# Transposes by the upper and lower half of the TensorE array, in a linear-attention and expert network

## The chip, the cores and the metric

The kernel runs on one core of one Trainium2 chip. The metric is the device time of one execution in microseconds (us). TensorE's matmuls are called PE here and its weight loads PEld; VectorE is DVE, ScalarE is ACT, GpSimd is POOL, and SP is the queue that issues the DMAs.

## The reference

Two kinds of layer alternate, A B A B, on x of 2048 tokens by 576 features, each with a layer norm ahead and a residual behind:

```python
x = x + A(layernorm(x), wqkv, wo)      # 32 heads of 18, linear attention
x = x + B(layernorm(x), w_q, k1, k2, u, v)
x = x + A(layernorm(x), wqkv, wo)
x = x + B(layernorm(x), w_q, k1, k2, u, v)

# A: q, k, v = x @ wqkv;  pq, pk = phi(q), phi(k)
#    kv = sum_s pk v^T;  z = sum_s pk;  o = (pq kv) / (pq z);  return o @ wo
# B: scores of 32 heads against 8 + 8 keys, best of each: one of 64 experts per head
#    return sum over heads of gelu(x . u[e]) * v[e]        (the softmax over one is 1)
```

Everything is fp32.

## The kernel before, in words

Tokens are worked on in 16 tiles of 128 (`NT`), so that a tile has its tokens on the 128 partitions and its features along the free axis. A matmul wants the features on the partitions, so each tile is transposed three times in each pair of layers: the layer-norm output before q, k and v (`front_T`, called `fT` in the written order, PSUM tile `ptf`), the scaled q features before the output product (`back_oT`, `oT`, `pto`), and the layer-norm output before the expert scores (`exp_T`, `bc`, `ptb`). `exp_T` also transposes the 128 x 128 tile of expert weights `cg` of an earlier token tile, mostly in the same call. All go through `transposed` (line 190): five blocks of 128 columns (`NB`), six with `cg`, each one `nc.tensor.transpose` (line 197) that loads the block of y, o or cg as the weights and streams the identity through, into columns of a PSUM tile of 1024 columns (two banks of 512). A second step, after a `yield`, splits the PSUM tile into `hi` and `lo` (`split`, lines 102 and 103): ACT writes the rounded fp32r copy, DVE the rest that it leaves. The products (`product` at line 212, `back_out` at 402, `exp_scores` at 433, `exp_out` at 517) then use `hi` and `lo` as weights in fp32r, so that three passes together give nearly fp32.

The other matmuls are `front_state` (lines 283 and 285, fp32, `kva`), which sums pk v^T over the tiles, and, in the first pass over the tiles, `fold_mm` (line 550), which multiplies the queries' weights by the keys. `fold_mm` is the one place where the array is used in parts: each of its weights has 32 columns, and four of them stand side by side in column groups of 32. In each tile of that stage, eight `fold_mm` come in one bunch.

The order of the work is written out by hand: `play` and `step2` list the pieces, `run` resumes a piece up to its next `yield`, and `in_order` ties every engine's instructions to that order. In the middle (`step2`, token tiles 5 to 12, one step for each) the first layer B of tile s, its output `po`, the second layer A's k and v of tile s - 3 and the transposes of tile s - 2 run in one step. There, `bc`, `fT` and `oT` stand near each other: `bc` and `fT` back to back on PE (eleven transposes), then `front_state`, then `oT` (five).

Of the kernel before, what the change touches and what calls it, by code (L numbers as in the profile page):

```python
# [22 lines left out]
P = 128  # L23
# [34 lines left out]
def network(ctx, tc, x_in, wqkv, wo, wq_t, k_t, u_t, v2, c_mask, c_mask4, c_ident, c_code, c_code1, c_scale, c_shift, out):  # L58
    nc = tc.nc
# [6 lines left out]
    def psum(name):  # L66
        return ps.tile([P, 1024], F32, tag="ps", name=name)
# [5 lines left out]
    ident = cp.tile([P, P], F32, name="ident")  # L73
# [26 lines left out]
    def split(src, hi, lo, eng=nc.vector):  # L100

        nc.scalar.activation(hi, src, AF.Copy)  # L102
        eng.tensor_tensor(lo, src, hi.bitcast(F32), op=ALU.subtract)  # L103
# [86 lines left out]
    def transposed(y, n, more=None, tag="t", step=P):  # L190

        todo = [y[:, b * step:b * step + P] for b in range(NB)] if y is not None else []
        todo += [] if more is None else [more]
        w = len(todo) * P
        pt = psum(f"pt{n}")
        for b, x in enumerate(todo):
            nc.tensor.transpose(pt[:, b * P:(b + 1) * P], x, ident)  # L197
        nb = NB if tag == "t" else NB + 1
        hi = wk.tile([P, nb, P], F32R, tag=tag + "hi", name=f"thi{n}", bufs=4 if tag == "t" else 1)
        lo = wk.tile([P, nb, P], F32R, tag=tag + "lo", name=f"tlo{n}", bufs=4 if tag == "t" else 1)  # L200
        yield
        split(pt[:, :w], hi.rearrange("p a b -> p (a b)")[:, :w], lo.rearrange("p a b -> p (a b)")[:, :w])
        return hi, lo

    def product(tt, hi, lo, cols, n, cut=HALF, rem=REM, by_block=False):
# [25 lines left out]
    def front_T(l, t):  # L231
        tt["f", l, t] = yield from transposed(ys.pop(("f", l, t)), f"f{l}_{t}")
# [151 lines left out]
    def back_oT(l, t):  # L384
        hi, lo = tt["oT", l, t] = yield from transposed(tt.pop(("o", l, t)), f"o{l}_{t}", step=HC)
        nc.gpsimd.tensor_copy(lo[96:112, 4], hi[:16, 4].bitcast(F32))
# [26 lines left out]
    def exp_T(l, t, c):  # L413

        y = ys.pop(("b", l, t)) if ok(t) else None
        cg = tt.pop(("cg", l, c)).rearrange("p a b -> p (a b)") if ok(c) else None
        if y is None and cg is None:
            return
        hi, lo = yield from transposed(y, f"b{l}_{t % 99}", cg, tag="t" if cg is None else "u")
        if y is not None:  # L420
            tt["b", l, t] = hi, lo
        if cg is not None:
            b = 0 if y is None else NB
            tt["c", l, c] = hi[:, b], lo[:, b]
# [426 lines left out]
```

## Time and profile before

| | |
|---|---|
| median of 3 runs | 755.47 us (755.28 to 756.19) |
| the profiled execution | 754.99 us, of which its span is 753.2 us |
| granted TensorE clock, mean | 0.999 |
| PE busy, PEld busy | 98%, 92% of the span |
| DVE, ACT, POOL busy | 61%, 38%, 26% |
| mean busy share of DMA queue 1 | 32% |

The span is the time from the first instruction to the last. PE is busy nearly throughout. Matmuls overlap in the profile: each lasts some 0.27 to 0.50 us from its start to its end, while the next starts 0.06 to 0.24 us after it. So what PE spends on one is read from the distance of the starts (called the pitch below), not from the duration. A weight load is shown with its own start; it runs beside the matmul before it. In a row of the timeline, the second number is the time from the start of the first instruction of a merged group to the end of its last.

### The profile page before, as it was taken

How to read it: one execution, taken by the hardware profiler on the slowest of the kernel's cores; microseconds unless marked ns; L12 is line 12 of the kernel's file. 1: busy time of each engine (PE TensorE's matmuls, PEld its weight loads, DVE VectorE, ACT ScalarE, POOL GpSimd, SP SyncE). 2: the span in 40 equal slices, each digit the busy share in tenths (PEclk: the TensorE clock that was granted, in tenths of full speed). 3: DMA queues.
4: the chain of work that ended last, by engine and by line, in shares of the span. 5: the costliest groups of instructions: out<-in, count | busy, mean ns of one | idle time of the engine just before them, and what ended most of it. 6: DMA issues, size and time to landing. Idle time of an engine off the chain costs nothing. (4 is left out here: it accounts for less than half of the span.)

```text
span 753.2 us, 13998 instructions
## 1 busy us (share of the span) xinstructions
PE 735.4 (98%) x5356; PEld 692.9 (92%) x5356; DVE 459.0 (61%) x1008; ACT 289.0 (38%) x586; POOL 197.1 (26%) x540
## 2 busy tenths in 40 slices
PE   7999999999999999999999999999999999999995
PEld 5999989999998989999999999999999999999984
DVE  5532342324246887666666666464366899899986
ACT  5422232232333544444444444353233333444343
POOL 2110001000002543333333333130033334533431
PEclk9999999999999999999999999999999999999999
DMA  9737446641111322322232212221734323121101
GB/s 272 248 100 243 162 169 220 220 119 49 48 63 32 111 84 82 98 84 83 87 103 105 88 67 76 90 72 51 187 86 118 103 83 114 32 84 44 48 33 63
DMA packets 52267, 79.48 MB, mean 106 GB/s; under 512 B 5480, under 2 KB 22376, under 8 KB 52200
## 3 DMA queue, kind: packets, MB, share of 16 engines
q1 hardware_dynamic: 52200, 78.59, 32.0%
q8 instruction: 42, 0.69, 0.4%
q14 instruction: 25, 0.20, 0.1%
HBM read 55.01 MB, written 23.56 MB: 104 GB/s over the span
## 5 line engine op out<-in xcount | busy, mean ns | idle before, releaser
L219 DVE TENSOR_SCALAR ek<-ek 128x576 f32<-128x576 f32 x32 | 14.7, 459 | 83.6 <-ACT ek L218 83.6
L212 PE MATMUL ppk<-whi,thif 128*128 128x288 f32 x320 | 50.2, 301 | 1.9 <-ACT thif L102 1.9
L402 PE MATMUL ppo<-ohi,thio 126*128 126x288 f32 (+1 forms) x320 | 50.7, 300 | 0.1
L212 PEld LDWEIGHTS ppk<-whi,thif 128*128 128x128 f32 x320 | 44.2, 188 | 5.9 <-issue 3.3
L163 POOL TENSOR_SCALAR rsf<-mvf 128x1 f32<-128x1 f32 x16 | 3.1, 192 | 175.7 <-DVE mvf L161 175.6
L212 PE MATMUL ppk<-whi,tlof 128*128 128x288 f32 x320 | 48.7, 296 | 0.2 <-DVE tlof L103 0.2
L219 DVE TENSOR_SCALAR eq<-eq 128x576 f32<-128x576 f32 x32 | 15.6, 488 | 54.2 <-ACT eq L218 54.2
L212 PE MATMUL ppv<-whi,thif 128*128 128x252 f32 x320 | 48.1, 296 | 0.1
L212 PE MATMUL ppv<-whi,tlof 128*128 128x252 f32 x320 | 47.6, 295 | 0.0
L187 ACT ACTIVATE yb<-x,rsb 128x640 f32<-128x640 f32 x32 | 29.5, 923 | 43.4 <-POOL rsb L180 43.3
L433 PE MATMUL pps<-shi,thib 128*128 128x512 f32 x160 | 44.0, 405 | 1.9 <-ACT thib L102 1.9
L402 PEld LDWEIGHTS ppo<-ohi,thio 126*128 126x128 f32 (+1 forms) x320 | 44.8, 189 | 0.9 <-DVE eq L221 0.3
L212 PEld LDWEIGHTS ppk<-whi,tlof 128*128 128x128 f32 x320 | 44.6, 188 | 0.5 <-DVE tlof L103 0.5
L212 PEld LDWEIGHTS ppv<-whi,tlof 128*128 128x128 f32 x320 | 44.7, 188 | 0.0
L212 PEld LDWEIGHTS ppv<-whi,thif 128*128 128x128 f32 x320 | 44.3, 188 | 0.4 <-ACT thif L102 0.3
L173 ACT ACTIVATE junk<-x,mb 128x576 bf16<-128x576 f32 x32 | 24.7, 771 | 49.7 <-POOL mb L172 46.4
L433 PE MATMUL pps<-shi,tlob 128*128 128x512 f32 x160 | 42.4, 395 | 0.0
L245 ACT ACTIVATE v<-ppv 128x252 f32<-128x252 f32 x64 | 20.9, 380 | 55.0 <-PE ppv L212 55.0
L218 ACT ACTIVATE eq<-ppq 128x576 f32<-128x576 f32 x32 | 20.7, 647 | 52.1 <-PE ppq L212 52.1
L212 PE MATMUL ppq<-whi 128*128 128x288 f32 x260 | 39.9, 300 | 0.6 <-DVE eq L221 0.6
L402 PE MATMUL ppo<-ohi,tloo 126*128 126x288 f32 x256 | 40.3, 295 | 0.0
L402 PE MATMUL ppo<-olo,thio 126*128 126x288 f32 x256 | 40.3, 296 | 0.0
(156 smaller groups left out, 1797.7 us busy)
## 6 DMA issues: line engine op xcount, KB each, us to landing
fold<-in_wq_t SPq DMA_DIRECT2D x64, 288.0 KB, 5.3
whi<-hl_d SPq DMA_DIRECT2D x26, 320.0 KB, 3.9
pq_d<-eq SPq DMA_DIRECT2D x19, 288.0 KB, 2.1
pq<-pq_d SPq DMA_DIRECT2D x19, 288.0 KB, 2.8
xf<-in_x SPq DMA_DIRECT2D x16, 288.0 KB, 5.6
x<-in_x SPq DMA_DIRECT2D x16, 288.0 KB, 2.8
x_d<-x SPq DMA_DIRECT2D x16, 288.0 KB, 3.0
x<-x_d SPq DMA_DIRECT2D x16, 288.0 KB, 2.8
```

The lines of the kernel that those rows point to most:

```text
L163: nc.gpsimd.tensor_scalar(rs[:, 0:1], mv[:, 1:2], EPS_LN, 1.0, op0=ALU.add, op1=ALU.mult)
L173: nc.scalar.activation(junk, xt, AF.Square, bias=m[:, 0:1], accum_out=m[:, 1:2])
L187: nc.scalar.activation(y, x2, AF.Identity, scale=rs[:, 0:1], bias=rs[:, 1:2])
L212: nc.tensor.matmul(o[:, at:at + c1 - c0], tt[a == "lo"][:, b, :], wb[:, cols + c0:cols + c1], start=(i == 0), stop=(i == len(todo) - 1))
L218: nc.scalar.activation(e.rearrange("p (b c) -> p b c", b=2), halves(p), AF.Exp)
L219: nc.vector.tensor_scalar(e, e, 1.0, EPS, op0=ALU.min, op1=ALU.add)
L245: nc.scalar.activation(vt[:, c * w:(c + 2) * w].rearrange("p (c e) -> p c e", c=2)[:, :, :HC], x.rearrange("p (c e) -> p c e", c=2), AF.Copy)
L402: nc.tensor.matmul(p[:, h * 512:h * 512 + HALF], hl[a][:r, b], w[:r, h * HALF:(h + 1) * HALF], start=(i == 0), stop=(i == len(todo) - 1))
L433: nc.tensor.matmul(p[:, :512], hl[a == "lo"][:, b, :], shi[:, b] if w == "hi" else slo[:, blocks(REM)[b][1]], start=(i == 0), stop=(i == l ...
```

## The change

The transposes of `transposed` are cut in two by token. Where one instruction transposed a block of 128 tokens by 128 features, there are now two, one for tokens 0 to 63 with the upper left 64 x 64 corner of the identity, one for tokens 64 to 127 with the lower right corner. Each loads 64 rows by 128 columns as weights, streams 64 columns, and gives 128 features by 64 tokens. Each stands in one half of the array's rows: in the built program these instructions have a tile of 64 rows by 128 columns at row 0 or 64, where all others but `fold_mm` have 128 by 128. The upper half writes into the first bank of the PSUM tile, the lower half into the second. The split reads the two banks as (half, block, 64) and writes `hi` and `lo` in their old layout, in runs of 64 elements. The transposes of `fold_T` (line 565) are left as they were, and the order of the pieces on every engine is the same.

```diff
         todo += [] if more is None else [more]
-        w = len(todo) * P
+        n_b = len(todo)
+
         pt = psum(f"pt{n}")
         for b, x in enumerate(todo):
-            nc.tensor.transpose(pt[:, b * P:(b + 1) * P], x, ident)
+            for h in range(2):
+                r = slice(64 * h, 64 * h + 64)
+                nc.tensor.transpose(pt[:, h * 512 + b * 64:h * 512 + b * 64 + 64], x[r], ident[r, r])
...
         yield
-        split(pt[:, :w], hi.rearrange("p a b -> p (a b)")[:, :w], lo.rearrange("p a b -> p (a b)")[:, :w])
+
+        def dst(x):
+            return x[:, :n_b].rearrange("p b (h t) -> p h b t", h=2)
+
+        split(pt.rearrange("p (h b t) -> p h b t", h=2, t=64)[:, :, :n_b], dst(hi), dst(lo))
         return hi, lo
```

## Rows read from the trace of the kernel before

**Rows 1.** The page, busy time of each engine, share of the span, instructions.
```profile
PE 735.4 (98%) x5356; PEld 692.9 (92%) x5356; DVE 459.0 (61%) x1008; ACT 289.0 (38%) x586; POOL 197.1 (26%) x540
```
**Rows 2.** Line 197: duration in ns, min/median/max, first and last start in us, shapes.
```profile
L197 PE MATMUL ptf<-ident,yf x160: 270/272/327, 7.2 to 524.4; 128*128 128x128 f32 x160
L197 PE MATMUL pto<-ident,o x160: 270/272/300, 237.0 to 722.5; 128*128 128x128 f32 x160
L197 PE MATMUL ptb<-ident,yb x160: 270/272/330, 249.0 to 736.8; 128*128 128x128 f32 x160
L197 PE MATMUL ptb<-ident,cg x32: 270/273/331, 265.7 to 747.7; 128*128 128x128 f32 x32
```
**Rows 3.** Timeline of PE in one middle step: start us, us, engine, line, operation, count.
```profile
337.88 0.71 PE L197 MATMUL ptb<-ident,yb 128*128 128x128 f32 x5
338.43 0.27 PE L197 MATMUL ptb<-ident,cg 128*128 128x128 f32 x1
338.54 0.71 PE L197 MATMUL ptf<-ident,yf 128*128 128x128 f32 x5
339.08 1.05 PE L283 MATMUL kva<-ek,v 128*127 128x126 f32 x8
...
340.10 0.71 PE L197 MATMUL pto<-ident,o 128*128 128x128 f32 x5
340.64 1.43 PE L433 MATMUL pps<-shi,thib 128*128 128x512 f32 x5
```
**Rows 4.** Timeline of PEld, loads of transposes after a wait.
```profile
300.40 0.14 PEld L197 LDWEIGHTS ptb<-ident,yb 128*128 128x128 f32 x1 [0.44 <-ACT yb L187]
300.46 0.25 PEld L197 LDWEIGHTS ptb<-ident,yb 128*128 128x128 f32 x2
```
**Rows 5.** Timeline of PE into and through a bunch of `fold_mm`, several narrow windows.
```profile
49.55 0.29 PE L285 MATMUL kva<-ek,v 128*73 128x72 f32 x2
49.62 0.23 PE L285 MATMUL kva<-ek,v 128*73 128x72 f32 x1
49.77 0.46 PE L550 MATMUL fold_ps<-fold,kpad 128*32 128x320 f32 x1
49.77 0.50 PE L550 MATMUL fold_ps<-fold,kpad 128*32 128x320 f32 x4
49.77 2.18 PE L550 MATMUL fold_ps<-fold,kpad 128*32 128x320 f32 x32
51.31 0.65 PE L550 MATMUL fold_ps<-fold,kpad 128*32 128x256 f32 x8
51.52 0.44 PE L550 MATMUL fold_ps<-fold,kpad 128*32 128x256 f32 x4
```
**Rows 6.** Timeline of PE and PEld out of that bunch, several narrow windows.
```profile
51.89 0.40 PE L212 MATMUL ppk<-whi,thif 128*128 128x288 f32 x1
51.89 0.19 PEld L212 LDWEIGHTS ppk<-whi,thif 128*128 128x128 f32 x1 [0.41 <-issue]
52.13 0.43 PE L212 MATMUL ppk<-whi,thif 128*128 128x288 f32 x2
52.13 0.56 PE L212 MATMUL ppk<-whi,thif 128*128 128x288 f32 x3
```
**Rows 7.** Waits of PEld: total us, times, longest us.
```profile
PEld ppk L212 <- issue: 3.3, 8, 0.4
```
**Rows 8.** Waits of PE: total us, times, longest us.
```profile
PE ptb L197 <- DVE cg L498: 2.5, 2, 1.7
PE pps L433 <- ACT thib L102: 1.9, 3, 1.0
```
**Rows 9.** ACT by line and shape: busy us, mean ns; idle before and its releaser.
```profile
L102 ACT ACTIVATE thif<-ptf 128x640 fp32r<-128x640 f32 x32 | 22.6, 706 | 10.0 <-PE ptf L197 10.0
L245 ACT ACTIVATE v<-ppv 128x252 f32<-128x252 f32 x64 | 20.9, 380 | 55.0 <-PE ppv L212 55.0
L572 ACT ACTIVATE shi<-fold_pt 128x112 fp32r<-128x112 f32 x20 | 4.8, 417 | 11.7 <-PE fold_pt L565 11.7
L102 ACT ACTIVATE thib<-ptb 128x128 fp32r<-128x128 f32 x5 | 1.4, 277 | 6.3 <-PE ptb L197 6.3
```

## The prediction

> **What bounds the kernel now.** I read the share of each engine first, then the transposes' own line, then the timeline of PE where transposes stand, and last the one place where the array already changes its partition. PE is busy 98% of the span with 5356 matmuls and no other engine is over 61% [rows 1], so what PE spends or saves is, to first order, time. PE's waits on other engines are few: the two largest sums are 2.5 and 1.9 us [rows 8].
>
> What a transpose costs is its pitch. In a middle step five transposes start at 337.88 and the next instruction at 338.43, five more at 338.54 and the next at 339.08 [rows 3]: 0.109 us each, and nothing ahead or behind, because PEld runs ahead of PE. There are 160 + 160 + 160 + 32 = 512 of them [rows 2], so 512 x 0.109 = 55.8 us, 7% of the span. In the written order of PE they stand in 81 unbroken runs: 45 of five, 15 of eleven, 13 of six, 4 of ten, 4 of one. The step of [rows 3] has an eleven and a five.
>
> The load of a transpose is quicker than its matmul: after a wait the first load starts at 300.40 and the second at 300.46 [rows 4], so one occupies PEld for about 0.059 us, and the matmul sets the pitch.
>
> **What the rows say of an array in parts.** `fold_mm` is the row nearest to what the change makes. Two things are seen. First, parts do work at the same time: four matmuls on four column groups start within 0.04 us (0.50 for four, 0.46 for one), and 32 matmuls of 320 and 256 columns are through in 2.18 us [rows 5]; the last four, of 256 columns, took 0.21 us each from 51.31 to 51.52, and 32 of those in a line would be 6.7 us. The loads of the four groups are hidden as well.
>
> Second, going into that partition and out of it costs PE time. In: the second L285 has 0.06 us of columns (0.29 for two, 0.23 for one), so PE is free at 49.68, but the first `fold_mm` starts at 49.77: 0.095 us lost [rows 5]. Out: the last `fold_mm` starts at 51.58 (0.44 for four, 0.38 for one), has 0.21 us of columns, and is done at 51.79. The next product's load starts only at 51.89, although its weights were ready, and the profile says "issue" for the 0.41 us in which PEld stood [rows 6]. The same stands 8 times, 3.3 us in all [rows 7], once per bunch. Since the load could not run ahead, it lies bare too: the second product matmul starts 0.24 us after the first, where the pitch is 0.13 (0.56 less 0.43) [rows 6]. So out costs 0.095 + 0.105 = 0.20 us.
>
> The Trainium skill, "TensorEngine Tiling (Array Packing)", section Key Properties, says that changing the tiling mode drains TensorE, and names no price; it speaks of every mode, a row mode too, and so against this change. By it the two losses above come at each run of transposes; without it they would not, which is the third rival below.
>
> **The change, part by part.** *Matmuls and loads:* 512 transposes become 1024, each half as many rows and half as many streamed columns, each with a load of 128 columns. If the halves work side by side as column groups do, a pair has the pitch of one half. No row shows a row group, so I bound the pair: from below by half of 0.109, 0.055 us, since 64 columns are streamed for 128; from above by two loads one after the other, 2 x 0.059 = 0.118. Between, the pair can't be quicker than a load, 0.059, if loads of a half set the pitch. I take 0.057, between 0.055 and 0.059, since in [rows 5] loads of different groups ran at once; the upper end is a rival. 512 x (0.057 - 0.109) = **-26.6 us**. The second half starts some 0.013 us after the first (0.04 for three more [rows 5]): 81 x 0.013 = **+1.1 us**.
>
> *Into the new partition,* 81 times: 0.095, and the first load bare, 0.059: 81 x 0.154 = **+12.5 us**. No row shows this for a half; the ends are nothing (0) and what `fold_mm` shows, and I take the latter, it being the only row.
>
> *Out of it,* 81 times: 0.095, and a bare load of the fp32 or fp32r operand behind, 0.105: 81 x 0.20 = **+16.2 us**, with the same ends.
>
> *Split:* ACT and DVE read two runs of PSUM and write ten or twelve runs of 64. Two runs cost ACT nothing: the v copy, 252 elements in two runs, is 380 ns, and the line through 277 ns for 128 elements and 706 for 640 gives 381 [rows 9]. Sixteen runs of seven scattered elements do cost: 417 ns for 112, where that line gives 264, so 0.0096 per run [rows 9]. For ten runs of 64 the ends are 0 and 0.1 us a split. I take 0, because 64 elements in one run are nearer to the v copy's 126 than to scattered ones. It would lie beside PE's other work except where PE waits for a split, as in [rows 8]; at worst I allow 3 us for it.
>
> *Order, queues, waits:* no piece moves on any engine, no DMA is added, and each run still waits for the same y, o or cg at its first load, and is released to ACT at its last matmul.
>
> *The sum:* -26.6 + 1.1 + 12.5 + 16.2 = +3.2 us. By the length of a run: a run of five saves 0.26 and pays 0.37, a run of eleven saves 0.57 and pays 0.37. Break-even is at seven, and 62 of 81 runs are shorter. Where PE stands anyway beside a run, a switch hides in the wait; I count some dozen such ends, 6 x 0.095 + 6 x 0.20 = 1.8 us. But time that a long run saves ahead of a wait is lost there too: in the middle step PE needs thib right behind the second run, and thib comes from ACT [rows 3, 8]. So I keep a third, -0.6. That makes **+2.6 us**: 757.6 against the profiled execution's 754.99, and 758.1 against the median, 755.47, which is 0.5 higher. I give 758.1.
>
> **Rivals.** *No pairing* (slower by much): the halves share one path for loads, so that the two loads of 0.059 come one after the other and the pair takes as long as the whole did, about 0.11. Then the body saves nothing and the switches are paid in full: 1.1 + 12.5 + 16.2 = 29.8, less about 4 that PE's waits swallow, so +26, about 781 us. It decides if the pair's pitch is over about 0.09. For it: only column groups are seen to load at once. Against it: nothing in the rows makes halves of the rows more alike than column groups. The Trainium skill, "TensorE: Matmul & The Clock Gate", section "LDWEIGHTS (loading the stationary operand)", says that a load's time goes by its columns and not by its rows, so that two loads of 64 rows are twice the work of one of 128; by it this rival is the outcome if loads do not pair, and the trace shows no load of fewer rows at the same columns to test it. Chance 0.20.
>
> *A pair in between,* 0.07 to 0.085, as the loads overlap in part: 512 x 0.02 = 10 more, about 766. Chance 0.09.
>
> *No drain, or a cheap one, for a row partition* (faster): the columns of a 64 x 128 tile leave the array as before, so that the switch costs little and loads run ahead. At 0 the body's -26.6 would be the whole change on PE, but the middle step can't use it, since there PE meets ACT's thib right behind the runs [rows 3, 8]; I keep 10 to 15 of it as an estimate: 740 to 746. Against: eight bunches, both ends, show the loss [rows 7]. The point from which it decides is a switch of in and out together below 0.31 us, where I count 0.354. At 0.07 instead of 0.095 for the drains the sum falls by 4.1 to -1.5, about 754. Chance 0.13.
>
> *The change does not do what it says* (a half is put through as a full tile, with neither pairing nor drain) would give the first rival's body without its switches, no change at all; the tile sizes in the built program speak against it, and I leave it inside the "same" chance.
>
> **How the numbers follow.** A measurement here tells 0.2%, 1.5 us, from no change. The forecast (pairs at 0.055 to 0.060, drains as in `fold_mm`) has 0.58; its own range is 753 to 763: the drains at 0.07 and the pair at 0.055 below, the split's 3 us and 0.060 above. In it lie 0.37 slower, 0.16 same, 0.05 faster. The no-pairing rival and the pair in between add 0.29 to slower. Cheap drains split 0.02 same and 0.11 faster. So slower 0.66, same 0.18, faster 0.16. The forecast's range alone holds under 0.6, so the range reaches up to the no-pairing rival: 752.8 to 782.
>
> **What would show it.** In the profile after: PE and PEld with 5868 instructions each; at a run of five pairs, about 0.29 us from the first of the ten to the last plus a tail; about 0.1 us between the end of the columns before and the first load of a run, and the same behind it, as "issue" waits at some 80 places; the second matmul behind a run 0.24 us after the first. L102 and L103 at their old 0.7 and 0.8 us. Wrong at once if ten halves take 0.5 us or more (no pairing), or if loads behind a run start before its last matmul (no drain).

## The result, and the profile after

The changed kernel takes 757.54 us (median of 16 runs), the kernel before 755.53 in the same measurement: a ratio of 1.0026, with a 95% interval of 1.0019 to 1.0032. It is 2.0 us slower, where 2.6 were forecast; the profiled execution has a span of 754.8 us.

The page, busy time of each engine, as in [rows 1]:

```profile
PE 736.3 (98%) x5868; PEld 677.9 (90%) x5868; DVE 459.0 (61%) x1008; ACT 288.0 (38%) x586; POOL 196.7 (26%) x540
```

PE and PEld have the 5868 instructions foreseen, and the other engines are where they were. The line of the transposes (now 200), against [rows 2]: 

```profile
L200 PEld LDWEIGHTS ptb<-ident,yb x320: 134/139/142, 250.3 to 738.4; 64*128 64x128 f32 x160
L200 PE MATMUL ptb<-ident,yb x320: 221/223/273, 250.3 to 738.5; 64*128 64x64 f32 x160
```

A load of 64 rows lasts as long as one of 128 did (median 139 ns; 0.14 us in [rows 4], and 140 ns as the median of line 197): the half has half the columns to stream, but a whole load.

The timeline of PE in the same middle step as [rows 3]:

```profile
339.51 0.53 PE L200 MATMUL ptb<-ident,yb 64*128 64x64 f32 x10
339.87 0.23 PE L200 MATMUL ptb<-ident,cg 64*128 64x64 f32 x2
339.93 0.47 PE L200 MATMUL ptf<-ident,yf 64*128 64x64 f32 x10
340.34 1.15 PE L290 MATMUL kva<-ek,v 128*127 128x126 f32 x8
341.32 0.29 PE L292 MATMUL kva<-ek,v 128*73 128x72 f32 x2
341.55 0.53 PE L200 MATMUL pto<-ident,o 64*128 64x64 f32 x10
342.17 0.51 PE L440 MATMUL pps<-shi,thib 128*128 128x512 f32 x1
```

From the first transpose to the state matmuls, the eleven now take 0.83 us, where they took 1.20. But the way in and the way out stand beside them. Narrow windows of the same stretch, PE and PEld:

```profile
339.26 0.31 PE L219 MATMUL ppv<-whi,tlof 128*128 128x324 f32 x1
339.50 0.13 PEld L200 LDWEIGHTS ptb<-ident,yb 64*128 64x128 f32 x1 [0.17 <-issue]
339.50 0.20 PEld L200 LDWEIGHTS ptb<-ident,yb 64*128 64x128 f32 x3 [0.17 <-issue]
339.51 0.27 PE L200 MATMUL ptb<-ident,yb 64*128 64x64 f32 x2
339.62 0.41 PE L200 MATMUL ptb<-ident,yb 64*128 64x64 f32 x7
...
340.12 0.29 PE L200 MATMUL ptf<-ident,yf 64*128 64x64 f32 x4
340.33 0.18 PEld L290 LDWEIGHTS kva<-ek,v 128*127 128x127 f32 x1
340.34 0.48 PE L290 MATMUL kva<-ek,v 128*127 128x126 f32 x2
```

**Pair.** The second pair starts at 339.62, the seventh (the first of ptf) at 339.93: 0.31 for five steps, 0.063 us a pair. The two matmuls of a pair start about 0.003 us apart: the first two take 0.27 us together, and one alone takes 0.27.

**In.** The last product matmul starts at 339.26; one of 324 columns takes 0.148 (the distance from such a start to the next among the product matmuls), so PE is free at 339.41. The first load starts at 339.50, 0.09 later, and it lies bare.

**Out.** The last half starts at 340.18 (0.29 for four, 0.22 for one) and has 0.053 of columns (a quarter of the 0.21 for 256 columns in [rows 5], an estimate), so it is through at 340.24. The next load starts at 340.33, again 0.097 later, and the second state matmul at 340.55 (0.48 for two, 0.27 for one), 0.21 behind the first, where it was 0.11 in the kernel before. This is the picture of `fold_mm` in [rows 5, 6], at a partition into row halves.

The waits of PEld show the way in at 57 of the 81 runs; the row of [rows 7] stands unchanged beside three others:

```profile
PEld ptb L200 <- issue: 6.3, 25, 1.9
PEld ppk L219 <- issue: 3.3, 8, 0.4
PEld pto L200 <- issue: 3.2, 13, 0.4
PEld ptf L200 <- issue: 3.2, 19, 0.2
```

They are 25 + 13 + 19 = 57 places with 12.7 us of "issue" ahead of the runs, some of it in waits that were there before. The prediction looked for some 80 places, and the same behind the runs; the pause behind a run is not in this list and is read from the starts alone.

The price of a run can be read without a model, from the start of the same matmul in the two profiles. For each of the 81 runs I took how much later the second matmul behind it starts, less how much later the last one ahead of it did:

| length of the run | runs | median change, us | sum, us |
|---|---|---|---|
| 1 | 4 | +0.19 (from -0.06 to +0.31) | +0.6 |
| 5 | 45 | +0.10 | +2.9 |
| 6 | 13 | +0.06 | +0.5 |
| 10 | 4 | -0.13 | -0.4 |
| 11 | 15 | -0.175 | -2.3 |

Together +1.3 us. Two of the fives stand in the first 15 us, at the warm-up matmuls and the first loads of weights, and make -1.1 of it, which I don't read as the price of a run: that stretch moves by as much without any change in it (the kernel with halves in the long runs, below, whose transposes are all whole up to 249 us, stands 1.2 us behind the kernel before at 30 us). From 30 us on, the runs add 2.3 us, the stretches between them take back 0.7, and the last matmul starts 1.6 us later.

All the lengths from five on agree on one price: with 0.046 saved per whole transpose, 0.10 + 5 x 0.046, 0.06 + 6 x 0.046 and 11 x 0.046 - 0.175 are each 0.33 to 0.34 us for a way in and out. Break-even is between seven and eight transposes.

### The profile page after: what moved, and what is told of

Read it like the earlier page. It is cut to its first block, busy times and chain, and to the rows that moved or that the text cites. A ratio compares the mean times of both kernels' runs of the same rounds, so it can differ in the third digit from the quotient of the medians.

```text
span 754.8 us, 15025 instructions
## 1 busy us (share of the span) xinstructions
PE 736.3 (98%) x5868; PEld 677.9 (90%) x5868; DVE 459.0 (61%) x1008; ACT 288.0 (38%) x586; POOL 196.7 (26%) x540
## 5 line engine op out<-in xcount | busy, mean ns | idle before, releaser
L398 DVE SCALAR_TENSOR_TENSOR x<-po,x 128x576 f32<-128x576 f32 x29 | 21.9, 754 | 30.8 <-PE po L524 29.7
L445 ACT ACTIVATE s<-pps 128x512 f32<-128x512 f32 x32 | 19.1, 596 | 56.2 <-PE pps L440 56.1
```

The costliest lines, as they stand in the source:

```text
L398: nc.vector.scalar_tensor_tensor(y.rearrange("p (b c) -> p b c", b=2), halves(p), 0.0, xt.rearrange("p (b c) -> p b c", b=2), op0=ALU.add, ...
L445: nc.scalar.activation(s[:, NE:], p[:, :512], AF.Copy)
```

## The experiments

The theory is that the change is the sum of a saving per transpose and a price per run of them. Its rivals are that the loss comes from the split's new order or from more instructions; that pairing is worth nothing; and that the way in and out costs nothing. Each kernel was timed beside the kernel before.

**The split alone.** Whole transposes, read in the new order:

```diff
-        split(pt[:, :w], hi.rearrange("p a b -> p (a b)")[:, :w], lo.rearrange("p a b -> p (a b)")[:, :w])
+        split(pt[:, :n_b * P].rearrange("p (b h t) -> p h b t", h=2, t=64), dst(hi), dst(lo))
```

> The kernel before with one edit: the split reads and writes in the order half, block, 64, from whole transposes. Theory (the change in time is the body of the transposes against the switches of the array's partition): the split costs nothing, L102 stays at 0.70 to 0.71 us for 640 elements and L103 at 0.82, and the time is that of before, 755.5 within 0.5. Rival (the 2 us come from the runs of 64 in the split): L102 or L103 longer, and about 757.5.

Measured: 755.63 us, a ratio of 0.9998 (0.9989 to 1.0007). ACT by line and shape, as in [rows 9]:

```profile
L102 ACT ACTIVATE thif<-ptf 128x640 fp32r<-128x640 f32 x32 | 22.6, 707 | 10.0 <-PE ptf L201 10.0
```

707 ns, where it was 706. The split's order is out as a cause, and the value 0 that was taken for it stands.

**Halves in the long runs only.** The 38 calls whose transposes stand in runs of ten or eleven are cut in halves, the other 63 are whole (`at` is the number of the call, in the order of PE, and LONG the list of the 38):

```diff
+        halved = at in LONG
+        if halved:
             for b, x in enumerate(todo):
                 for h in range(2):
                     r = slice(64 * h, 64 * h + 64)
                     nc.tensor.transpose(pt[:, h * 512 + b * 64:h * 512 + b * 64 + 64], x[r], ident[r, r])
+        else:
+            for b, x in enumerate(todo):
+                nc.tensor.transpose(pt[:, b * P:(b + 1) * P], x, ident)
```

> Halves only in the 19 unbroken runs of ten or eleven transposes; whole transposes in the 62 shorter runs. Theory: with the pair at 0.063 us as the changed kernel's profile has it, a run of eleven saves 11 x 0.046 = 0.51 and pays 0.35 for its two switches, a run of ten saves 0.46; 15 x 0.16 + 4 x 0.11 = 2.8 us faster than before, about 752.7. Rival (the loss is per transpose or per split, from more instructions or from the split's order): 38 of 101 calls are changed, so 0.38 x 2.0 = 0.8 us slower than before, about 756.3.

Measured: 753.94 us, a ratio of 0.9975 (0.9965 to 0.9985), 1.8 us faster than before. The sign is the theory's, and the opposite of the rival's. A part of the 2.8 is given back. PEld in the middle step:

```profile
339.27 0.39 PEld L208 LDWEIGHTS ptf<-ident,yf 64*128 64x128 f32 x10
339.73 0.96 PEld L305 LDWEIGHTS kva<-ek,v 128*127 128x127 f32 x8
340.61 0.25 PEld L307 LDWEIGHTS kva<-ek,v 128*73 128x73 f32 x2
340.78 0.53 PEld L211 LDWEIGHTS pto<-ident,o 128*128 128x128 f32 x5
341.54 0.53 PEld L455 LDWEIGHTS pps<-shi,thib 128*128 128x128 f32 x3 [0.23 <-DVE tlob L103]
```

DVE's tlob ahead of the scores, first in this kernel, then in the kernel before:

```profile
340.54 0.95 DVE L103 TENSOR_TENSOR tlob<-ptb,thib 128x768 fp32r<-128x768 f32 x1
```

```profile
339.63 0.95 DVE L103 TENSOR_TENSOR tlob<-ptb,thib 128x768 fp32r<-128x768 f32 x1
340.64 1.00 PEld L433 LDWEIGHTS pps<-shi,thib 128*128 128x128 f32 x5
```

The scores wait for tlob, which ACT and DVE make from the first of these transposes: of the 0.175 us, about 0.07 is lost there again in seven of the eight steps, and nearly all of it in the one shown. The kernel before already stood at this limit. Its load of the scores starts at 340.64, 0.05 after tlob's end, as here, and does so in all eight steps; its second score matmul starts 0.34 us after the first, where the pitch is 0.23. So the load lies bare behind the five transposes of oT before they are halved, and part of the price of their way out was paid already.

**Halves in the short runs only.** The same with `at not in LONG`.

> The complement: halves only in the 62 runs of one, five or six; whole transposes in the 19 long ones. Theory: a run of five pays 0.10 to 0.12 net, one of six 0.07, one of one 0.30, so 45 x 0.11 + 13 x 0.07 + 4 x 0.30 = 7.1 us, less 1 to 2 that lie in waits of PE: 5 to 6 slower than before, about 761. Together with the long runs it gives the whole change's +2. Rival (per transpose or split): 0.62 x 2.0 = 1.2 us slower, about 756.7.

Measured: 758.85 us, 1.0040 (1.0027 to 1.0052): 3.1 us slower. The theory has the sign and the rival's 1.2 is below the interval, but the size is under the 5 to 6 expected: more of these runs lie beside waits of PE than I allowed. Measured as in the table above, the 62 runs add 4.4 us from 30 us on, where 7.1 were counted; the eight fives ahead of the scores add 0.02 to 0.07 apiece. With the long runs, -1.8 + 3.1 = +1.3, against +2.0 for the whole change; the intervals cover the difference. In the profiles, from 30 us on, the last matmul starts 1.5 us earlier with the long runs and 3.5 later with the short ones, together +2.0, against +1.6 with all.

**Both halves on one side of the array.** The tokens 0 to 63 are transposed in the place of 64 to 127 too:

```diff
-                r = slice(64 * h, 64 * h + 64)
+                r = slice(0, 64)
```

> The changed kernel with both halves of each block on the upper half of the array: the tokens 0 to 63 are transposed twice and the tokens 64 to 127 not at all, so the output is not the reference's; instructions, shapes, banks and switches are the same in number. Theory (the halves work side by side, and one after another each takes the 0.063 us of a pair): 512 x 0.063 = 32 us more than the changed kernel, less some 5 in waits of PE, about 784. Rival (pairing is worth nothing, halves are quick because they are small): the time of the changed kernel, 757.5.

Measured: 783.74 us, 1.0369 (1.0354 to 1.0383). PE in the middle step:

```profile
346.99 0.83 PE L200 MATMUL ptb<-ident,yb 64*128 64x64 f32 x10
347.67 0.28 PE L200 MATMUL ptb<-ident,cg 64*128 64x64 f32 x2
347.79 0.78 PE L200 MATMUL ptf<-ident,yf 64*128 64x64 f32 x10
```

From the first half of cg to the first of ptf are 0.12 us for two halves, where a pair took 0.06. So the pairing is real, and worth 26 us here; without it a half costs more than half a whole transpose (0.063 against 0.109). The no-pairing rival of the prediction had put its time at about this (781).

**Every run broken once more.** A whole transpose whose result nobody reads is put into each call of five or six blocks:

```diff
+            if b == 2:
+                nc.tensor.transpose(pt[:, 384:512], x, ident)
```

> The changed kernel, with one whole transpose of the third block put behind its two halves in each of the 96 calls with five or six blocks, into columns that nobody reads: every run is broken by one more way out of the partition and one more way in. Theory: 0.097 + 0.058 + 0.107 for the whole one and 0.097 + 0.058 for the way back, less 0.01, is 0.41 us a call; 96 x 0.41 = 39 us, less some 4 in waits: about 792. Rival (no price at the switch of the partition): the whole one's own 0.109, 96 x 0.109 = 10.5 us, about 768.

Measured: 790.02 us, 1.0457 (1.0441 to 1.0473), 34.7 above before and 32.5 above the changed kernel: 0.34 us for each of the 96 calls. Of it 0.11 is the whole transpose itself, so one more way out and in costs 0.23, net of what PE's waits swallow. That is less than the 0.33 of the table; about half of the difference is that the load that lies bare behind the way out is here that of a transpose (0.059 [rows 4]) and not that of an operand (0.105). PE at one such place:

```profile
350.12 0.40 PE L200 MATMUL ptb<-ident,yb 64*128 64x64 f32 x6
350.45 0.33 PE L202 MATMUL ptb<-ident,yb 128*128 128x128 f32 x1
350.71 0.34 PE L200 MATMUL ptb<-ident,yb 64*128 64x64 f32 x4
```

The third pair starts at 350.30 (0.40 for six, less 0.22 for one, after 350.12), the whole one 0.15 later, and the next pair 0.26 after that. The price is paid where the partition changes, at every change, and is not one of the transposes being halved.

**The five of oT joined to the eleven.** To pay one way in and out for sixteen, oT goes ahead of the state matmuls in the eight middle steps; once with halves in the long runs, the sixteens among them, and once whole, as a control:

```diff
-        run(1, (v, s - 3), (fT, s - 2), (keep, s - 2 if s - 2 < 13 else -1), (st, s - 3))
-        run(0, (oT, s + 1), (S, s), (gel, s, 1), (po, s - 1, 3), (gel, s), (sel, s, 2), (po, s - 1), (O, s + 1), (sel, s),
+        run(1, (v, s - 3), (fT, s - 2))
+        run(0, (oT, s + 1))
+        run(1, (keep, s - 2 if s - 2 < 13 else -1), (st, s - 3))
+        run(0, (S, s), (gel, s, 1), (po, s - 1, 3), (gel, s), (sel, s, 2), (po, s - 1), (O, s + 1), (sel, s),
```

> The long-runs kernel with one piece moved: in the eight middle steps the transposes of the scaled q features stand right behind those of the layer-norm output, ahead of the state matmuls, so that each step has one run of sixteen in halves in place of a run of eleven in halves and one of five whole. ACT, DVE, POOL and SP keep their orders. Theory: the five go over to halves without a switch of their own, 8 x 5 x 0.046 = 1.8 us less than the long-runs kernel, about 752.1. Rival (the five then wait for a free PSUM tile or for o, as they stand 1.1 us earlier): what they wait eats it, up to 8 x 0.6 us, 754 to 757.

> The same move alone, with all transposes whole: the control for the run before. Theory: no switch is saved because there is none, so the time of before, 755.6 within 0.7. Rival (the five wait in their earlier place, or the later state matmuls help or hurt by themselves): a time away from before by over 1 us, and a wait at L197 pto in the middle steps.

Measured: 758.49 us with halves, 1.0040 (1.0028 to 1.0053), and 761.04 whole, 1.0079 (1.0065 to 1.0092), beside 755.33 for the kernel before. The rivals have the direction in both, and 758.49 is above the 754 to 757 given: the move itself costs 5.7 us. The waits of PEld with halves, then whole:

```profile
PEld pto L208 <- ACT v L270: 7.0, 8, 0.9
```

```profile
PEld pto L201 <- ACT v L257: 5.7, 8, 0.7
```

In its earlier place oT waits for a copy of v by ACT, eight times; the last copy of v is what empties a PSUM tile in the kernel's text, while the profile names the copy alone. That the halves are 2.5 us better than whole at this place fits the theory (8 steps, 16 x 0.046 - 0.33 = 0.41 less a longer wait, and the other long runs), but the version is no use. Whether an earlier copy of v would free it was not tried, as the copy would delay thib and with it tlob, for which the scores already wait.

**Upper halves first.**

```diff
-        for b, x in enumerate(todo):
-            for h in range(2):
+        for h in range(2):
+            for b, x in enumerate(todo):
```

> The changed kernel with the instructions of a call in the order: all upper halves, then all lower halves, in place of upper and lower in turn. If each half of the array takes its own instructions ahead of those of the other, as the column groups of fold_mm did: pairs as before, 757.5 within 1. If matmuls start in the written order alone, so that only neighbours pair: ten halves one after another at 0.063 in most calls, up to 512 x 0.063 = 32 us more, 780 to 785.

Measured: 766.84 us, 1.0150 (1.0136 to 1.0164): between the two. PE in the middle step:

```profile
342.27 0.40 PE L203 MATMUL ptb<-ident,yb 64*128 64x64 f32 x3
342.27 0.45 PE L203 MATMUL ptb<-ident,yb 64*128 64x64 f32 x4
342.63 0.22 PE L203 MATMUL ptb<-ident,cg 64*128 64x64 f32 x1
342.69 0.22 PE L203 MATMUL ptb<-ident,yb 64*128 64x64 f32 x1
342.69 0.22 PE L203 MATMUL ptf<-ident,yf 64*128 64x64 f32 x1
342.75 0.22 PE L203 MATMUL ptb<-ident,yb 64*128 64x64 f32 x1
```

Three halves start alone before a fourth matmul joins them, within 0.01 us of the third. Halves on one side start 0.06 apart in the kernel above, so this must be the first lower one, which the call of six blocks has in seventh place. Later a ptf of the next call starts beside a ptb of this one, ahead of ptb's last. So a half does not wait for everything written ahead of it; why the first lower one does not start at once is not shown. (The four first matmuls of a bunch of `fold_mm` start within 0.04 us [rows 5], though each of its eight pieces is four matmuls, so that the fourth to start is written thirteenth.) The written order, upper and lower in turn, is part of what the change is worth.

## Why the prediction was right, by its steps

*The bound.* PE was the bound, and what it saved or spent became time, except beside waits.

*The body.* The pair was put at 0.057 us between 0.055 and 0.059 and measures 0.063, just above: 512 x (0.063 - 0.109) = -23.6 us in place of -26.6. The term was mis-sized by 3.0 us, because I took the pair to be bound by the longer of load and columns alone. In the profile, each pair's loads start a few ns after the matmuls of the pair ahead, and its matmuls about 0.054 after that; so the load and the step to it set the pitch, not the 0.053 of columns. This is read from the order of the starts; no run changes the load alone.

*The switches.* In and out are there at every run, with the 0.09 to 0.10 us that `fold_mm` had shown for another kind of partition: read from the starts as above, the pause is at least 0.086 us ahead of each of the 81 runs, and 0.096 behind. That choice, at the end of a range that began at 0, carried the sign. By the table a run pays 0.33, where the prediction had 0.367 with its tail: 81 x 0.33 = 26.7 in place of 29.8. The 0.013 between the halves is 0.003 in fact, which takes back 0.8 of a tail of 1.1 us. The bare first load costs 0.047 and not 0.059, as the second pair starts 0.11 us after the first where the pitch is 0.063: 1.0 us more. The rest I can't place. What PE does in the pause of 0.09 to 0.10 us is not shown.

*The sum.* -23.6 + 26.7 = +3.1, against +3.2: two errors of 3 us cancelled. For the waits I took off 0.6; 2.0 measured leaves 1.1, and the profiles' 1.6 leaves 1.5. The wait that I named for the middle step was the wrong one: the three waits for thib of [rows 8] stand at 303.4, 723.1 and 738.2 us, outside the eight middle steps, and in these the scores wait for DVE's tlob. That a long run's gain is partly lost ahead of the scores was right. The total's closeness is in part luck; the sign was not, as each of the two terms and the break-even near seven are confirmed by kernels that change one of them.

*The rivals.* No pairing: refuted by the pitch; the kernel on one side of the array, which does without it, takes 783.7. A pair in between: refuted too, the pitch being 0.063 and not 0.07 or more (its 766 should have been 768, 10 above 758.1). No drain in a row partition: refuted by the rows, and by the 0.23 us that a further break costs beside its own transpose. The sentence of the Trainium skill, "TensorEngine Tiling (Array Packing)", section Key Properties, that a change of tiling mode drains TensorE held for the row mode here, at 0.09 to 0.10 us from the end of the columns to the next load. The statement of the Trainium skill, "TensorE: Matmul & The Clock Gate", section "LDWEIGHTS (loading the stationary operand)", that rows don't shorten a load, agrees with 139 ns for 64 rows and 140 for 128; it did not decide, since the loads of the two halves run together. The prediction was wrong that the trace of the kernel before has no load of fewer rows to test it:

```profile
L314 PEld LDWEIGHTS z<-kvb,pick x16: 186/192/192, 229.2 to 541.3; 127*128 127x128 f32 x16
L315 PEld LDWEIGHTS z<-kvb,pick x4: 190/191/192, 230.0 to 541.6; 73*128 73x128 f32 x4
```

Here 73 rows by 128 columns take 191 ns and 127 rows 192.

## What to carry to other kernels

Work that uses part of the array pays for each change of the partition, here 0.33 us for in and out, most of which is a pause plus a weight load that can't be made ahead; so count the unbroken runs of such work, not its instructions, and use it only in runs past the break-even (seven to eight transposes here; halves in the long runs alone were 1.8 us faster than the kernel before, and 3.6 faster than the change as made). Look for the price of a mode in the one place of the trace that already uses one; here that was another mode, and the prices agreed. Before moving pieces to make a run longer, look at which PSUM tile the moved piece needs, and what empties it.

## What the runs showed of the hardware that was not expected

A load of 64 rows and 128 columns takes as long as one of 128 rows (the kernel before shows it for 73 rows), and two of them on the two halves of the array take no longer than one; so pairs of transposes stand at the pitch of their loads (0.063 us) and not of their columns (0.053, an estimate). Between the halves, matmuls start out of their written order within a few instructions: in the kernel with the upper halves first, the first lower half starts as the fourth of a call of six blocks, where it was written seventh. And the pause at a change of the partition was the same, 0.09 to 0.10 us, into column groups, out of them, into row halves and out of those.
